# A blocked attention and two mixture layers on one core: one late exponential per half unit, the float64 conversion paused at the change of layers

## The chip, the cores and the metric

The kernel runs on 1 core of one Trainium2 chip. The metric is device microseconds from launch to end; three timed executions of the kernel before took 914.43, 926.68 and 923.3 us, median 923.3 us. A further execution was profiled.

## What is computed

Attention over blocks with 8 memory keys and a local window, then two feed-forward layers of 1536 tokens x 512. The first has four experts weighted by normalised domain probabilities and a ReLU, the second a hidden size of 2048 with a per-channel leaky slope:

```python
scores = scale * np.matmul(q_c, k_full.transpose(0, 1, 3, 2))
scores = scores - np.max(scores, axis=-1, keepdims=True)
a = np.exp(scores)
a = a / (np.sum(a, axis=-1, keepdims=True) + 1e-09)
out[:, :, c_start:c_end] = np.matmul(a, v_full)
...
h = np.maximum(x @ w1[e], 0.0)
out += p[:, e:e + 1] * (h @ w2[e])
...
h = x @ w_in
g = np.maximum(h, 0.0) + alpha * np.minimum(h, 0.0)
return (g @ w_out).astype(np.float32)
```

The weights of the second layer (`w_in`, `w_out`) arrive as float64 bit patterns and are turned into float32 on the chip.

## The kernel before

**Attention.** The work is 16 units (a batch entry and a block of 96 queries), each in two half units of 4 heads, so 32 half units, numbered 0 to 31 in the order in which they run. A half unit is a generator (`half_unit`, line 191) of four stages. Stage 1: four score products `s` on TensorE into one PSUM bank (96 queries x 4 heads x 128 keys), the next load of queries and keys, the row maximum `mx` and its scaled negative `nm` on VectorE, four exponentials `pe` on ScalarE (line 213, one for each head, reading PSUM, with `nm` as bias). Stage 2: four transposes `t` on TensorE and a copy `pt_ring` on ScalarE. Stage 3: four products `x` with the values (a column of ones gives the sums), then on VectorE `dn`, `rd` and the scaled result `xs_ring`. Stage 4: two transposes `xt` and a copy into `acc` on ScalarE; after every fourth half unit `prep_x` (line 128) makes the sums `st` and the high and low parts `xh` and `xl` of 96 columns for the products that follow. `pe`, `pt_ring` and `xs_ring` have two buffers each, used by half units in turn.

**Order.** Everything on TensorE, VectorE, ScalarE and GpSimd is kept in the order in which Python emits it (`Pinned`, line 47; line 57 is therefore the line of almost every instruction). That order comes from a planner's clock `now`, which each matmul moves on by its supposed duration. A generator that yields `LAT` is called again when `now` has passed that time; at most `LIVE` = 4 half units are open, a new one each `PACE` = 2.3. While nothing else can be run (`att_poll(force=True)`), small bf16 matmuls on a tile `warm` fill the gap (`fill`, line 92). The first 20 half units run like this; the rest are put between the matmuls of the first column tile's second product (`product`, line 448).

**Layers.** Each layer is a loop over 256 hidden channels (pair p = 0 to 15 in the first, 16 to 23 in the second) and over two column tiles of 384. `gemm1` (line 455) is seven products of six matmuls (`a`, `b`, `d`, `a`, `c`, `d`, `c`) from the sums of inputs and of weights, `gemm2` (line 542) eight outputs `y` of six, added into `acc` by VectorE (`evac`). Operands are float32 split into a high part (`xh`, `wh`, `gg`) cast by ScalarE and a low part (`xl`, `wl`, `gg`) subtracted by GpSimd, or by VectorE for p = 0 and 1 (`fast`). `prep_w` (line 298) makes the weights ahead of need; where TensorE's turn comes first, `prep_force` (line 425) emits the missing steps on the spot.

**Conversion.** `convert` (line 373) turns the second layer's weights into float32 in 32 chunks, one each 18 of the planner's clock: load into the tile tagged `fr`, five VectorE instructions on `fm` and `fw`, one on ScalarE and two on GpSimd (`fl`), a store to the DRAM tile `w2s`. `prep_w` loads the raw weights of pair p only once chunk 4(p-15) has been emitted (`conv_done`).

**Change of layers.** When `gemm2` of pair 15 has finished a column tile, `transition` (line 155) runs `prep_x` four times over it with VectorE for `st` and `xl`, while the other column tile is multiplied. The order of tiles there is written out in line 607.

Of the kernel before, what the change touches and what calls it, by code (L numbers as in the profile page):

```python
# [10 lines left out]
F32 = mybir.dt.float32  # L11
# [3 lines left out]
AF = mybir.ActivationFunctionType  # L15
ALU = mybir.AluOpType
# [4 lines left out]
BLK = 96  # L21
NCH = BLK // CH
KEYS = MEM + LEFT + BLK + RIGHT
DQ = D + NCH
NBLK = S // BLK
NU = B * NBLK
NT, DM = B * S, H * D
E, F1, F2 = 4, 1024, 2048
P = 128
# [33 lines left out]
def tile_kernel(ctx: ExitStack, tc: tile.TileContext, qk, mask, v, wa, wq, dpt, alpha, out):  # L63
    nc = tc.nc
    scale = 1.0 / float(D) ** 0.5
    pe_, dve, act, pool = (Pinned(tc, e) for e in (nc.tensor, nc.vector, nc.scalar, nc.gpsimd))

    cp = ctx.enter_context(tc.tile_pool(name="cp", bufs=1))
# [21 lines left out]
    now = [0.0]  # L90
# [34 lines left out]

    acc = xp.tile([P, KD, 2, NCOL], F32, name="acc")

    def prep_x(c0, n, fast):
        cs = slice(c0, c0 + n)
        b11, b12 = acc[:, 0:2, 0, cs], acc[:, 0:2, 1, cs]  # L130
        b21, b22 = acc[:, 2:4, 0, cs], acc[:, 2:4, 1, cs]
        st = bp.tile([P, 4, 2, n], F32, tag="st", name=f"st{c0}")
        e = dve if fast else pool
        sub = ALU.subtract
        act.copy(xh[:, 0:4, cs], acc[:, :, 0, cs])
        e.tensor_tensor(out=st[:, 0], in0=b12, in1=b11, op=sub)
        yield
        e.tensor_tensor(out=st[:, 1], in0=b22, in1=st[:, 0], op=sub)
        act.copy(xh[:, 4:6, cs], b22)
        yield  # L140
        e.tensor_tensor(out=st[:, 2], in0=b22, in1=b12, op=sub)
        pool.tensor_tensor(out=xl[:, 0:4, cs], in0=acc[:, :, 0, cs], in1=xh[:, 0:4, cs].bitcast(F32), op=sub)
        yield
        e.tensor_tensor(out=st[:, 3], in0=b21, in1=st[:, 1], op=sub)
        pool.tensor_tensor(out=xl[:, 4:6, cs], in0=b22, in1=xh[:, 4:6, cs].bitcast(F32), op=sub)
        yield
        for z in (0, 2):
            r = slice(6 + 2 * z, 10 + 2 * z)
            t_ = st[:, z:z + 2].rearrange("p a b n -> p (a b) n")
            act.copy(xh[:, r, cs], t_)  # L150
            yield
            e.tensor_tensor(out=xl[:, r, cs], in0=t_, in1=xh[:, r, cs].bitcast(F32), op=sub)
            yield
# [37 lines left out]
    def half_unit(u, half):  # L191

        hu = 2 * u + half
        tq, tv = qk_t[hu % RING], v_t[hu % RINGV // 2][:, hu % 2]
        tq = tq[:DQ]
        qv = tq[:, :QW].rearrange("p (h q) -> p h q", q=BLK)
        kv = tq[:, QW:].rearrange("p (h k) -> p h k", k=KEYS)
        vv = tv.rearrange("p (h d) -> p h d", d=D + 1)
        c, ab = divmod(u, 2)
        cols = slice(c * BLK, (c + 1) * BLK)  # L200
        hs = slice(2 * half, 2 * half + 2)
        nm = f"{u}_{half}"
        s_ps = bank(f"s{nm}").rearrange("p (h k) -> p h k", k=KEYS)
        for i in range(4):
            mm(s_ps[:BLK, i], qv[:, i], kv[:, i], n=KEYS, passes=4, start=True, stop=True)
        load_half(hu + RING)
        mx = cp.tile([P, 4], F32, tag="mx", bufs=4, name=f"mx{nm}")
        dve.tensor_reduce(out=mx[:BLK], in_=s_ps[:BLK], axis=AX.X, op=ALU.max)
        nm_ = cp.tile([P, 4], F32, tag="nm", bufs=4, name=f"nm{nm}")
        dve.tensor_scalar_mul(nm_[:BLK], mx[:BLK], -scale)  # L210
        pe = pe_t[hu % 2]
        for i in range(4):
            act.activation(
                pe[:BLK, i], s_ps[:BLK, i], AF.Exp, bias=nm_[:BLK, i:i + 1], scale=scale
            )
        yield LAT[0]
        t_ps = bank(f"t{nm}")[:, :4 * BLK].rearrange("p (h q) -> p h q", q=BLK)
        for i in range(4):
            pe_.transpose(t_ps[:, i], pe[:BLK, i], ident[:BLK, :BLK])
            now[0] += 0.085  # L220
        pt = pt_ring[:, hu % 2]
        act.copy(pt, t_ps)
        yield LAT[1]
        x_ps = bank(f"x{nm}")[:, :4 * (D + 1)].rearrange("p (h d) -> p h d", d=D + 1)
        for i in range(4):
            mm(x_ps[:BLK, i], pt[:, i], vv[:, i], n=D, passes=4, least=0.17, start=True, stop=True)
        load_v(hu + RINGV)
        dn = cp.tile([P, 4, 1], F32, tag="dn", bufs=2, name=f"dn{nm}")
        dve.tensor_scalar_add(dn[:BLK], x_ps[:BLK, :, D:D + 1], 1e-9)
        rd = cp.tile([P, 4, 1], F32, tag="rd", bufs=2, name=f"rd{nm}")  # L230
        dve.reciprocal(rd[:BLK], dn[:BLK])
        xs = xs_ring[:, hu % 2]
        dve.tensor_tensor(
            out=xs[:BLK], in0=x_ps[:BLK, :, :D], in1=rd[:BLK].to_broadcast([BLK, 4, D]),
            op=ALU.mult,
        )
        yield LAT[2]
        xt_ps = bank(f"xt{nm}")[:, :2 * BLK].rearrange("p (c q) -> p c q", q=BLK)
        xf = xs.rearrange("p h d -> p (h d)")
        for z in range(2):  # L240
            pe_.transpose(xt_ps[:, z], xf[:BLK, z * P:(z + 1) * P], ident[:BLK, :BLK])
            now[0] += 0.085
        act.copy(acc[:, hs, ab, cols], xt_ps)
        if ab == 1 and half == 1:
            for _ in prep_x(c * BLK, BLK, c < 2):
                yield 0.4

    att = {"next": 0, "start": 0.0, "done": 0, "over": set(), "live": []}

    def att_poll(force=False):  # L250

        while True:
            due = [x for x in att["live"] if x[0] <= now[0]]
            room = att["next"] < 2 * NU and len(att["live"]) < LIVE
            if due:
                x = due[0]
                try:
                    lat = next(x[1])
                    x[0] = now[0] + lat
                except StopIteration:  # L260
                    att["live"].remove(x)
                    att["over"].add(x[2])
                    while att["done"] in att["over"]:
                        att["done"] += 1
            elif room and att["start"] <= now[0]:
                g = half_unit(*divmod(att["next"], 2))
                att["start"] = now[0] + (PACE0 if force else PACE)
                att["next"] += 1
                x = [0.0, g, att["next"] - 1]
                att["live"].append(x)  # L270
                x[0] = next(g) + now[0]
            elif force:
                times = [x[0] for x in att["live"]]
                if room:
                    times.append(att["start"])
                t = min(times)
                fill(int((t - now[0]) / 0.11))
                now[0] = max(now[0], t)
                continue
            else:  # L280
                return
            if force:
                return
# [81 lines left out]
    def convert():  # L365

        for k in range(4 * NP2):
            t0 = now[0]

            def pause(t=DT_CONV):  # L370
# [254 lines left out]
    for i, (what, k) in enumerate(order):  # L625
        p, c0, n = tiles[k]
        if what == 1:
            if p == 0:
                while att["done"] < 4 * -(-(c0 + n) // BLK):
                    att_poll(force=True)  # L630
                    prep_poll()
                    if att["next"] >= 4 and not second:
                        second = True
                        load_raw(0, 1)
                        nc.sync.dma_start(nalpha, alpha)
                    if att["done"] >= 4 and not pb_t:
                        gate()
                        dve.tensor_scalar_mul(nalpha, nalpha, -1.0)
                        load_pb(0, 0, FIRST[0][1])
            if k == k0:  # L640
                stream("c", convert())
                streams["c"][0] = now[0] + 20.0
            if k + 1 < len(tiles):
                p1, d0, m = tiles[k + 1]
                if p1 < NP1 and (2 * p1 * P // F1, d0, m) not in pb_t:
                    load_pb(2 * p1 * P // F1, d0, m)
            if p >= NP1 and f"x{c0}" in streams:
                prep_force(f"x{c0}", lambda: f"x{c0}" not in streams)
            hold[0] = p == 0
            acts[k] = gemm1(p, c0, n, k % 2 if p else 0, k == final[p])  # L650
        else:
            hold[0] = False
            gemm2(p, c0, n, acts.pop(k), order[i - 1] == (1, k), k == final[p])
            if p == NP1 - 1:
                stream(f"x{c0}", transition(c0, n))
# [2 lines left out]
USE = (A11, S2, S1, A12, S3, S4, A22)  # L658
SLOTS = 10

LAT = (2.6, 1.0, 1.4)
LIVE = 4
PACE = 2.3
PACE0 = 2.3
# [80 lines left out]
```

## Time and profile before

| | |
|---|---|
| timed executions | 914.43, 926.68, 923.3 us (median 923.3) |
| profiled execution, its own time | 916.23 us |
| its span (first to last instruction) | 914.5 us |
| lies around the span | 1.7 us |
| mean granted TensorE clock | 0.972 |
| busy: PE, DVE, ACT, POOL | 870.7, 622.9, 363.0, 571.2 us |

PE is TensorE's matmuls, PEld its weight loads, DVE VectorE, ACT ScalarE, POOL GpSimd. PE is busy 95% of the span, but the share is not the same everywhere: the span falls into attention (0 to 148 us, with the first pair's products from 76.8 us on), the first layer (to 621 us), the change of layers (621 to 677 us) and the second layer. The granted clock is given as a share of 2.4 GHz, so that 0.5 is 1.2 GHz, and a mean of 0.82 over a stretch is 36% of it at the lower level.

### The profile page before, as it was taken

To read this page: it belongs to the slowest core of one execution; us is meant where nothing else is said; L and a number is where in the kernel's file an instruction comes from. 1 tells how busy PE (TensorE), PEld (TensorE's weight loads), DVE (VectorE), ACT (ScalarE), POOL (GpSimd) and SP (SyncE) were. 2 spreads that over 40 slices of the span, in tenths; PEclk is the share of its full clock that TensorE was granted. 3 is DMA by queue.
4 is the path that set the end of the run, shared out by engine and by line. 5 is a ranking of instruction groups with operands and counts; after the bars stand their busy time and mean duration, and the time that the engine had idled before them with its cause. 6 is when DMAs were issued, how large, how long until landed. Compare 5 with 4: busy or idle time off the path is not lost.

```text
span 914.5 us, 14418 instructions
## 1 busy us (share of the span) xinstructions
PE 870.7 (95%) x5211; PEld 852.5 (93%) x5211; DVE 622.9 (68%) x1232; ACT 363.0 (40%) x874; POOL 571.2 (62%) x619
## 2 busy tenths in 40 slices
PE   8888779999999999999999999998689999999998
PEld 7778668999999999999999999997579999999998
DVE  4765444676777677767766676769987767765655
ACT  4655343222323232322232232324456556454632
POOL 1134333677768776777777787767559778775521
PEclk9789888999999999999999999999889999999999
DMA  7442220022223213321232223121102221211003
GB/s 187 127 146 70 65 78 24 24 70 92 79 72 104 72 56 100 120 70 59 81 105 73 89 81 104 47 82 42 61 15 101 93 80 37 87 53 47 1 1 138
DMA packets 29353, 69.36 MB, mean 76 GB/s; under 512 B 4536, under 2 KB 12856, under 8 KB 29282
## 3 DMA queue, kind: packets, MB, share of 16 engines
q1 hardware_dynamic: 29186, 68.41, 23.2%
q8 instruction: 41, 0.67, 0.3%
q14 instruction: 30, 0.25, 0.1%
q0 software_dynamic: 96, 0.03, 0.0%
HBM read 56.87 MB, written 11.56 MB: 75 GB/s over the span
## 4 chain that ended last, share of the span: by engine, by line
PE 86%; DVE 6%; ACT 4%; issue 1%; POOL 1%; DMA 1%; SPq 0%; ACTq 0%; DVEq 0%; POOLq 0%
PE y L57 42%; PE a L57 10%; PE d L57 10%; PE c L57 10%; PE b L57 5%; PE s L57 3%; PE x L57 3%; ACT pe L57 2%; DVE st L57 2%; DVE xl L57 1%; DVE mx L57 1%; PE t L57 1%; ACT pt_ring L57 1%; DVE g L57 1%; DMA qk<-in_mask 1%
## 5 line engine op out<-in xcount | busy, mean ns | idle before, releaser
L57 PE MATMUL y<-gg,wh 128*128 128x384 f32 x1540 | 404.8, 338 | 8.2 <-POOL gg L57 3.9
L57 PEld LDWEIGHTS y<-gg,wh 128*128 128x128 f32 x1540 | 280.7, 190 | 12.2 <-POOL gg L57 6.2
L57 POOL TENSOR_TENSOR gg<-g,gg 128x384 fp32r<-128x384 f32 x192 | 198.9, 1044 | 128.9 <-ACT gg L57 105.8
L57 PE MATMUL y<-gg,wl 128*128 128x384 f32 (+1 forms) x770 | 259.9, 337 | 0.0
L57 DVE TENSOR_TENSOR acc<-y,acc 128x384 f32<-128x384 f32 x353 | 188.5, 550 | 66.8 <-PE y L57 63.6
L57 ACT CAST gg<-g 128x384 fp32r<-128x384 f32 x192 | 97.6, 511 | 168.9 <-DVE g L57 168.7
L57 PEld LDWEIGHTS y<-gg,wl 128*128 128x128 f32 x770 | 146.2, 190 | 0.0
L57 POOL TENSOR_TENSOR wl<-raw,wh 128x256 fp32r<-128x256 f32 (+1 forms) x110 | 109.2, 1003 | 50.1 <-PE b L57 43.1
L57 ACT COPY u<-a 128x384 f32<-128x384 f32 x48 | 23.0, 479 | 215.9 <-PE a L57 215.7
L57 POOL TENSOR_TENSOR wl<-s,wh 128x256 fp32r<-128x256 f32 x88 | 67.7, 777 | 5.1 <-ACT wh L57 5.0
L57 PE MATMUL c<-xh,wh 128*128 128x384 f32 x192 | 64.9, 338 | 4.3 <-DVE b L57 4.3
L57 PE MATMUL d<-xh,wh 128*128 128x384 f32 x192 | 64.8, 337 | 0.6 <-DVE t L57 0.6
L57 PE MATMUL d<-xh,wl 128*128 128x384 f32 x192 | 64.6, 336 | 0.0
L57 PE MATMUL c<-xl,wh 128*128 128x384 f32 x192 | 64.6, 336 | 0.0
L57 PE MATMUL c<-xh,wl 128*128 128x384 f32 x192 | 64.6, 336 | 0.0
L57 PE MATMUL d<-xl,wh 128*128 128x384 f32 x192 | 64.6, 336 | 0.0
L57 PE MATMUL a<-xh,wh 128*128 128x384 f32 x192 | 64.5, 336 | 0.0
L57 PE MATMUL a<-xl,wh 128*128 128x384 f32 x192 | 64.4, 335 | 0.0
L57 DVE TENSOR_TENSOR u<-b,u 128x384 f32<-128x384 f32 x48 | 26.7, 556 | 55.2 <-PE b L57 51.2
L57 PE MATMUL a<-xh,wl 128*128 128x384 f32 x192 | 64.2, 334 | 0.0
L57 POOL TENSOR_TENSOR xl<-acc,xh 128x384 fp32r<-128x384 f32 (+1 forms) x32 | 27.6, 868 | 51.5 <-ACT xh L57 51.4
L57 ACT ACTIVATE pe<-s,nm 96x128 f32<-96x128 f32 x128 | 36.1, 360 | 58.0 <-DVE nm L57 41.5
(142 smaller groups left out, 1591.2 us busy)
## 6 DMA issues: line engine op xcount, KB each, us to landing
raw<-in_wa SPq DMA_DIRECT2D x32, 512.0 KB, 3.4
fr<-in_wq SPq DMA_DIRECT2D x32, 512.0 KB, 3.4
w2s<-fl SPq DMA_DIRECT2D x32, 256.0 KB, 2.8
raw<-w2s SPq DMA_DIRECT2D x16, 512.0 KB, 3.6
qk<-in_qk SPq DMA_DIRECT2D x32, 224.0 KB, 3.4
v<-in_v SPq DMA_DIRECT2D x32, 130.0 KB, 2.1
pb<-p_dram SPq DMA_DIRECT2D x8, 384.0 KB
outT<-acc SPq DMA_DIRECT2D x15, 192.0 KB, 2.0
```

Source lines behind the costliest of these rows:

```text
L57: return self.tc.keep_in_program_order(f(*a, **kw))
```

## The change

Three things are edited. (1) In a half unit the scaled negative maximum and the four exponentials go. VectorE subtracts the maximum from all 4 x 128 scores at once, from PSUM into the `pe` buffer in SBUF; after a further yield of `LATE` = 1.5 one exponential runs in place over 96 x 512. `LAT` becomes (1.2, 1.5, 1.6). `clear` holds a half unit back until the one two before it, whose buffers it takes over, has emitted the stage that frees them. (2) `convert` begins no chunk while `change[0]` is true, from `gemm2` of tile kx-2 to `gemm2` of tile kx+1 (the change of layers). (3) In that stretch every second `prep_x` takes its `st` from the tile tagged `fr`, which the conversion otherwise uses.

```diff
-        st = bp.tile([P, 4, 2, n], F32, tag="st", name=f"st{c0}")
+        st = bp.tile([P, 4, 2, n], F32, tag="fr" if change[0] and c0 // n % 2 else "st", name=f"st{c0}")
...
-        nm_ = cp.tile([P, 4], F32, tag="nm", bufs=4, name=f"nm{nm}")
-        dve.tensor_scalar_mul(nm_[:BLK], mx[:BLK], -scale)
         pe = pe_t[hu % 2]
-        for i in range(4):
-            act.activation(
-                pe[:BLK, i], s_ps[:BLK, i], AF.Exp, bias=nm_[:BLK, i:i + 1], scale=scale
-            )
+        dve.tensor_tensor(
+            out=pe[:BLK], in0=s_ps[:BLK], in1=mx[:BLK].unsqueeze(2).to_broadcast([BLK, 4, KEYS]),
+            op=ALU.subtract,
+        )
+        yield LATE
+        act.activation(pe[:BLK], pe[:BLK], AF.Exp, scale=scale)
         yield LAT[0]
...
+    NEED = {0: 3, 2: 4, 3: 5}
+
+    def clear(hu):
+        return hu < 2 or att["stage"][hu - 2] >= NEED.get(att["stage"][hu], 0)
...
-            due = [x for x in att["live"] if x[0] <= now[0]]
-            room = att["next"] < 2 * NU and len(att["live"]) < LIVE
+            due = [x for x in att["live"] if x[0] <= now[0] and clear(x[2])]
+            room = att["next"] < 2 * NU and len(att["live"]) < LIVE and clear(att["next"])
...
         for k in range(4 * NP2):
+            yield now[0], lambda: not change[0]
...
             hold[0] = False
+            change[0] = kx - 2 <= k <= kx + 1
...
-LAT = (2.6, 1.0, 1.4)
+LAT = (1.2, 1.5, 1.6)
+LATE = 1.5
```

How the edit moves instructions is seen at three places. The first is TensorE in the second part of attention, where half units stand between the matmuls `y` of pair 0 (`s`, `t`, `x`, `xt` as above; the number behind a name counts tiles, so equal numbers are the same half unit's stage). Before:

```order
L57 MATMUL x_1_1272<-v_107,pt_ring 96x65 x4
L57 MATMUL s_1_1284<-qk_106 96x128 x4
L57 MATMUL t_0_1298<-ident,pe_110 128x96 x4
L57 MATMUL y_0_1_1_0_1270<-gg_0_0_1122,wl_0_658 128x384
L57 MATMUL xt_1_1305<-ident,xs_ring 128x96 x2
L57 MATMUL y_0_1_1_0_1270<-gg_0_0_1122,wh_0_657 128x384
L57 MATMUL y_0_0_0_0_1140<-gg_0_0_1138,wh_0_657 128x384
L57 MATMUL y_0_0_0_0_1140<-gg_0_0_1138,wl_0_658 128x384
L57 MATMUL y_0_0_0_0_1140<-gg_0_0_1138,wh_0_657 128x384
L57 MATMUL x_0_1314<-v_108,pt_ring 96x65 x4
L57 MATMUL s_0_1325<-qk_104 96x128 x4
L57 MATMUL t_1_1339<-ident,pe_111 128x96 x4
```

So `x` of one half unit was followed by the scores of the half unit two later, then by the transposes of the one between. Now:

```order
L57 MATMUL s_1_1278<-qk_105 96x128 x4
L57 MATMUL x_1_1287<-v_108,pt_ring 96x65 x4
L57 MATMUL t_0_1298<-ident,pe_110 128x96 x4
L57 MATMUL y_0_3_0_0_1149<-gg_0_0_1063,wl_0_552 128x384
L57 MATMUL y_0_3_0_0_1149<-gg_0_0_1063,wh_0_551 128x384
L57 MATMUL y_0_0_1_0_1187<-gg_0_0_1059,wh_0_551 128x384
L57 MATMUL s_0_1309<-qk_106 96x128 x4
L57 MATMUL xt_1_1318<-ident,xs_ring 128x96 x2
L57 MATMUL x_0_1325<-v_107,pt_ring 96x65 x4
L57 MATMUL t_1_1338<-ident,pe_111 128x96 x4
```

The scores of the half unit two later now stand ahead of `x`, and those of the half unit three later behind it.

The second place is ScalarE in the same stretch. Before, the exponential of the next half unit stands ahead of the copy `pt_ring` of this one:

```order
L57 ACTIVATE pe_111<-s_1_1284,nm_1_1292 96x128 x4
L57 COPY pt_ring<-t_0_1298 128x384
L57 COPY acc<-xt_1_1305 128x2x96
L57 ACTIVATE pe_110<-s_0_1325,nm_0_1333 96x128 x4
L57 COPY pt_ring<-t_1_1339 128x384
```

Now, with the exponential on `pe` in place:

```order
L57 ACTIVATE pe_111<-pe_111 96x512
L57 COPY pt_ring<-t_1_1262 128x384
L57 COPY acc<-xt_0_1268 128x2x96
L57 ACTIVATE pe_110<-pe_110 96x512
L57 COPY pt_ring<-t_0_1298 128x384
```

The copy is that of the same half unit whose exponential stands ahead of it (`pe_111` and `t_1`, `pe_110` and `t_0`).

The third place is ScalarE at the last pair's first column tile (`gemm1` of p = 23), where the conversion's later end shows. Before, all casts of that pair's weights `wh_23` stand ahead of `u`:

```order
L57 CAST wh_23_2_9488<-raw_23_9183 128x256
L57 CAST gg_22_384_9468<-g_22_384_9431 128x384
L57 CAST gg_22_384_9476<-g_22_384_9475 128x384
L57 CAST wh_23_9516<-raw_23_9246 128x512 x2
L57 COPY u_0_9566<-a_0_9558 128x384
L57 ACTIVATE g_23_0_9591<-a_0_9558 128x384
L57 ACTIVATE g_23_0_9591<-g_23_0_9591,nalpha 128x384
L57 ACTIVATE g_23_0_9610<-b_0_9568 128x384
```

Now the last three casts stand among the products' own work:

```order
L57 COPY u_0_9452<-a_0_9442 128x384
L57 CAST wh_23_5_9473<-s_9318 128x256
L57 ACTIVATE g_23_0_9481<-a_0_9442 128x384
L57 ACTIVATE g_23_0_9481<-g_23_0_9481,nalpha 128x384
L57 CAST wh_23_6_9494<-s_9318 128x256
L57 ACTIVATE g_23_0_9505<-b_0_9454 128x384
L57 ACTIVATE g_23_0_9505<-g_23_0_9505,nalpha 128x384
L57 CAST wh_23_2_9510<-raw_23_9250 128x256
```

The casts of the sixth and seventh weight sets (`wh_23_6`, `wh_23_2`) moved behind ScalarE's work on the products `a` and `b` of the same `gemm1`.

## Rows read from the trace of the kernel before

**Rows 1.** Stretches: start:end, length, busy PE, PEld, DVE, ACT, POOL, clock, DMA share, GB/s.

```profile
15.30:31.70 16.40, 13.88 (x112) 12.89 (x113) 12.41 (x36) 10.61 (x37) 1.69 (x2) 0.83 0.40 108
31.70:63.10 31.40, 27.54 (x222) 25.39 (x221) 20.75 (x62) 18.23 (x59) 7.45 (x10) 0.82 0.53 146
63.10:76.80 13.70, 10.50 (x108) 9.85 (x106) 6.65 (x20) 9.13 (x30) 5.34 (x8) 1.00 0.39 109
76.80:92.40 15.60, 13.70 (x100) 13.32 (x100) 8.42 (x21) 7.84 (x24) 7.25 (x10) 1.00 0.23 63
92.40:147.80 55.40, 44.84 (x317) 39.53 (x316) 21.69 (x64) 21.77 (x72) 15.78 (x22) 0.82 0.21 59
...
168.50:604.30 435.80, 435.80 (x2515) 435.65 (x2514) 313.78 (x589) 131.38 (x292) 321.95 (x338) 1.00 0.24 80
...
621.00:677.00 56.00, 40.89 (x182) 35.76 (x181) 52.43 (x89) 25.48 (x59) 39.61 (x40) 0.88 0.14 47
...
691.70:894.50 202.80, 202.80 (x1172) 202.80 (x1171) 134.63 (x251) 106.89 (x231) 134.79 (x145) 1.00 0.15 52
```

**Rows 2.** Waits of PE from 0 to 165 us: total, times, longest.

```profile
PE x L57 <- ACT pt_ring L57: 20.4, 17, 1.9
```

**Rows 3.** The chain that ended last, 107.7 to 112.5 us: start, us, what.

```profile
107.80 0.89 PE x L57 x8
108.70 0.92 PE s L57 x8
...
109.64 0.70 DVE mx L57
...
110.43 0.18 DVE nm L57
...
110.71 0.13 ACT pe L57
...
110.98 0.86 ACT pe L57 x3
111.84 0.37 ACT pt_ring L57
...
112.25 0.30 PE x L57
```

**Rows 4.** Groups of instructions by form: busy us, mean ns, idle before.

```profile
L57 DVE TENSOR_TENSOR acc<-y,acc 128x384 f32<-128x384 f32 x351 | 187.8, 551 | 66.4 <-PE y L57 63.3
...
L57 ACT ACTIVATE fl<-fr 128x512 f32<-128x512 uint32 x32 | 21.5, 672 | 4.4 <-POOL fl L57 4.4
```

**Rows 5.** The chain that ended last, at 146 us: twelve warm matmuls.

```profile
146.32 1.31 PE ps98.54266666666673_1721 L57 x12
```

**Rows 6.** Timeline of VectorE and of GpSimd around 625 us: start, duration.

```profile
625.02 0.55 DVE L57 TENSOR_TENSOR xl<-st,xh 128x384 fp32r<-128x384 f32 x1
...
625.96 1.17 DVE L57 TENSOR_TENSOR xl<-st,xh 128x384 fp32r<-128x384 f32 x1
...
625.23 1.48 POOL L57 TENSOR_TENSOR fl<-fl,fm 128x512 f32<-128x512 f32 x1 [1.42 <-PE a L57]
```

**Rows 7.** Stretch 621 to 677 us, tile `fm` alone: DVE busy, POOL busy, clock, DMA.

```profile
621.00:677.00 56.00, 4.37 (x7) 2.74 (x2) 0.88 0.14 47
```

**Rows 8.** The same stretch, tile `fl` alone: ACT busy, POOL busy, clock, DMA.

```profile
621.00:677.00 56.00, 0.69 (x1) 5.44 (x4) 0.88 0.14 47
```

**Rows 9.** The tile `fw` over the span: ns min/median/max, first and last start.

```profile
L57 DVE SCALAR_TENSOR_TENSOR fw<-fr,fm x32: 674/730/1349, 200.5 to 794.2; 128x512 uint32<-128x512 uint32 x32
```

**Rows 10.** ScalarE's timeline in the last pair's first tile: start, duration.

```profile
875.86 0.49 ACT L57 ACTIVATE g<-a 128x384 f32<-128x384 f32 x1 [2.64 <-PE a L57]
...
878.08 0.62 ACT L57 ACTIVATE g<-g,nalpha 128x384 f32<-128x384 f32 x1
```

**Rows 11.** TensorE's timeline there, first product with the sixth set's low part.

```profile
877.05 0.33 PE L57 MATMUL d<-xh,wl 128*128 128x384 f32 x1
```

**Rows 12.** GpSimd's low parts of weights, by form: busy us, mean ns, idle before.

```profile
L57 POOL TENSOR_TENSOR wl<-s,wh 128x256 fp32r<-128x256 f32 x88 | 67.7, 777 | 5.1 <-ACT wh L57 5.0
```

More of the change, by code (lines that the diff above doesn't have):

```diff
@@ L126, in tile_kernel @@
     acc = xp.tile([P, KD, 2, NCOL], F32, name="acc")
+    change = [False]
     def prep_x(c0, n, fast):
@@ L246, in half_unit @@
                 yield 0.4
-    att = {"next": 0, "start": 0.0, "done": 0, "over": set(), "live": []}
+    att = {"next": 0, "start": 0.0, "done": 0, "over": set(), "live": [], "stage": [0] * 2 * NU}
+    NEED = {0: 3, 2: 4, 3: 5}
+    def clear(hu):
+        return hu < 2 or att["stage"][hu - 2] >= NEED.get(att["stage"][hu], 0)
     def att_poll(force=False):
         while True:
-            due = [x for x in att["live"] if x[0] <= now[0]]
-            room = att["next"] < 2 * NU and len(att["live"]) < LIVE
+            due = [x for x in att["live"] if x[0] <= now[0] and clear(x[2])]
+            room = att["next"] < 2 * NU and len(att["live"]) < LIVE and clear(att["next"])
             if due:
@@ L257, in att_poll @@
                 try:
+                    att["stage"][x[2]] += 1
                     lat = next(x[1])
@@ L271, in att_poll @@
                 x[0] = next(g) + now[0]
+                att["stage"][x[2]] = 1
             elif force:
-                times = [x[0] for x in att["live"]]
+                times = [x[0] for x in att["live"] if clear(x[2])]
                 if room:
```

## The prediction

> **What bounds the kernel now.** I read the busy time by stretch first. In the two layers TensorE has no gap at all: 435.8 of 435.8 us and 202.8 of 202.8 us busy, at a granted clock of 1.00 [rows 1]. Nothing that the change does to other engines can make these 639 us shorter; it can only spoil them. All that is to be had lies in attention (15.3 to 147.8 us) and at the change of layers (621 to 677 us). There the clock is 0.82 to 0.88 in most stretches, and TensorE is idle besides.
>
> Next the waits. In attention TensorE waits for one thing, the copy `pt_ring` ahead of the value products: 20.4 us in 17 waits, none over 1.9 us [rows 2]. Then the chain, to see why that copy is late. From one `x` to the next, 107.80 to 112.25, is 4.45 us, and the chain goes through everything: `x` 0.89, `s` 0.92, `mx` 0.70, `nm` 0.18, the exponentials, `pt_ring` 0.37, `x` again [rows 3]. The order rows say why it is a circle: `s` of the half unit two later stands behind `x`, and its exponential stands ahead of the `pt_ring` of the half unit between. So each half unit costs one whole circle of 4.45 us, whatever TensorE could do.
>
> At the change of layers VectorE is the bound: 52.43 of 56.0 us busy, TensorE 40.89 [rows 1]. 4.37 us of VectorE and 5.44 us of GpSimd there are the conversion's [rows 7, 8].
>
> **The change, part by part.**
>
> *The subtraction.* No row shows it. `mx` reads the same 96 x 512 from PSUM in 0.70 us [rows 3]; a two-input instruction with one input in PSUM takes 0.551 us for 384 columns [rows 4]. Scaled by columns the latter gives at most 0.73 for 512. Below I bound it by 0.55, above by twice 0.70, since two-input instructions are sometimes doubled (0.55 and 1.17 us for the same `xl`) [rows 6]. It is nearest to `mx`; I take 0.69. The second `xl` began while GpSimd's `fl` of 1.48 us ran. The Trainium skill ("SBUF — State Buffer", Who interferes with whom) says that a VectorE instruction with two SBUF inputs is held by a GpSimd instruction that reads SBUF, and one with a single SBUF input is not. The rows agree for `xl`; the subtraction has one input in PSUM, so by that rule it stays near 0.69, while the doubled price would lower the gain by the 12 us worked out below.
>
> *The exponential.* Four took 1.13 us from the first's start at 110.71 (0.86 for the last three) [rows 3]. One over 512 columns lies between 0.86 and the 0.672 us of a 512-column activation [rows 4], or below that since it follows an in-place source of fewer partitions; I take 0.62, with 0.5 and 0.86 as bounds. ScalarE gets about 0.4 us free per half unit, but it is not the bound anywhere. `mx`, subtraction and exponential together (0.70 + 0.69 + 0.62) last as long as before (0.70 + 0.18 + 1.13): the change of instructions by itself gains nothing and costs VectorE 0.51 us for each half unit (0.69 for 0.18).
>
> *The order.* This is where the gain is. In the order rows of after, `x` stands ahead of the scores of the half unit three later, and each `pt_ring` behind its own exponential only. The circle becomes `x`, `s`, `mx`, subtraction, exponential, `t`, `pt_ring`, `x`: 0.89 + 0.92 + 0.70 + 0.69 + 0.62 + 0.37 [rows 3], 0.45 for four transposes (no row shows them; half of `x`'s eight matmuls) and 0.25 of gaps (what the 4.45 us leave over their parts) = 4.9 us, but now once in three half units, 1.6 us each. That is below what TensorE needs for one, so TensorE becomes the bound where VectorE isn't.
>
> *Second part of attention (76.8 to 147.8, 71.0 us).* TensorE's own work: 13.70 us at clock 1.00, and 44.84 at 0.82. A mean of 0.82 over 55.4 us is 36% at the lower level, 19.9 us, of which half (10.0) is stretch. At full clock 13.7 + 34.9 = 48.6 us. The order has 14 more warm matmuls in this part (78 for 64) at 1.31 / 12 = 0.11 us [rows 5]: 1.5 us. Floor 50 us. I take 55, since the last two or three half units have nothing beside them and still run as a chain. Gain 16 us; bounds 0 (a circle of 4.45 us stays) and 21.
>
> *First part (15.3 to 76.8, 61.5 us, half units 4 to 19).* TensorE 13.88 + 27.54 + 10.50 = 51.9 us, of it (0.34 x 16.4 + 0.36 x 31.4) / 2 = 8.4 stretch: 43.5, with 4 more warm matmuls 44. VectorE, which also prepares the first pairs' weights here: 12.41 + 20.75 + 6.65 = 39.8, plus 16 x 0.51 = 8.2: 48 us. Both floors lie close together and the order can't fill both, so I take 52. Ten more warm matmuls stand ahead of the fifth scores: 1 us. Gain 9.5 - 1 = 8.5 us; bounds 0 and 12.5. With a subtraction of 1.4 us VectorE's floor would be 59.5, and nearly all of this part's gain is gone; the second part would lose some 4 us as well: 12 us together.
>
> *Change of layers.* With the conversion paused, 4.37 us leave VectorE's chain and 5.44 us GpSimd. The second also shortens `xl` and `st`, as seen above. What is late next are ScalarE's casts `xh` and GpSimd's `xl`. The second `st` buffer gives nothing: VectorE writes `st` and reads it last, in its own order. I take 5 us; bounds 0 (another engine's chain of the same length) and 56.0 - 48.1 = 8.
>
> *Where the chunks go.* One chunk comes about every 19 us ((794.2 - 200.5) / 31) [rows 9]; nine now follow the change of layers (nine of the 32 stand behind it in the order), to about 850 us in the old time. In the second layer TensorE has no gap, with VectorE at 134.63 and GpSimd at 134.79 of 202.8 us [rows 1], so 3 more chunks of about 3.1 us of VectorE each (4.37 / 7 for one of a chunk's five instructions [rows 7]) are covered. If they were not, each would cost up to that. What isn't covered is the end: raw weights of pair 23 wait for the last chunk, and the order puts the casts of its sixth and seventh sets behind ScalarE's work on `a` and `b`. In old time `a` gets its first activation at 875.86 to 876.35 and the second (0.62, as the one at 878.08) to 876.97; then come the cast of 256 columns (at most the 0.49 of 384 columns, I take 0.4) and GpSimd's low part of 0.777: 878.15 [rows 10, 12], where TensorE wants it at 877.05 [rows 11]: 1.1 us. The seventh: ScalarE is done with `b` at 878.70, then again 0.4 + 0.78 = 879.88, wanted one set later (six matmuls of 435.8 / 2515 = 0.173 us [rows 1]), at 878.09, and the 1.1 of delay: 0.7 us more. Cost 1.8 us; bounds 0 and 5 (each of the last four sets late by cast and subtraction). Queues of DMA: the load of pair 23 stands in SP's order ahead of the last two stores, so it isn't held by them.
>
> **Sum.** -8.5 - 16 - 5 + 1.8 = -27.7 us. The profiled span was 914.5, so 886.8, and with 1.7 us around it 888.5 us against that execution's own 916.2. The median of the runs shown is 923.3, 7 us above; I add 2.5 us for such scatter: 891 us.
>
> **Rivals.** *VectorE takes over*: the subtraction costs near 1.4 us. For it: VectorE's doubled rows, and a floor of 48 us already next to TensorE's 44. Against: `acc<-y,acc`, also with one PSUM input, averages 0.551 us over 351 [rows 4], with GpSimd busy beside it. 891 + 12 = 903 us.
>
> *The circle stays*: some other pair of instructions ties each half unit to the one before in the second part, as `exp` and `pt_ring` did. For it: VectorE's and ScalarE's orders still mix half units. Against: the order rows. 891 + 16 = 907 us.
>
> *The clock goes, slower than before*: TensorE works at 1.2 GHz through attention. For it: it was at 0.82 there with TensorE busy 81 to 88% [rows 1]. Against: in the layers, without gaps, it is 1.00, and the new order has fewer gaps. Each us of full-clock work at the lower level costs 1 us more; attention has 44 + 50 = 94, and I left 4 and 5 us for all delays. It decides from 28 + 9 = 37 us of stretch, 40% of that work at the lower level (about 20% now: 18.4 of 94). At 60%, 56 - 37 = 19 us over: 935 us.
>
> *The pause does nothing*: casts and GpSimd are the chain at the change of layers. 896 us.
>
> **Chances.** Forecast with the pause's rival 0.68 (876 to 900 us: from all gains at their floors, 41.5 us less 1.8, to 9 us short of the sum). VectorE 0.13, circle 0.13, clock 0.06. The range of 876 to 911 leaves out the clock and half of the scatter. A measurement of this kernel can tell about 2%, so faster is below 904.8: the forecast and part of the VectorE case, 0.72; same 0.23; slower than 941.8: 0.05.
>
> **What would show it.** Right: `PE x <- ACT pt_ring` falls from 20.4 to under 8 us; the clock of attention is above 0.9; the last `xt` of attention at 118 to 127 us; `mx` and subtraction back to back on VectorE in 1.4 us; the change of layers some 51 us; a wait of TensorE of 1 to 2 us for `wl` or `wh` near the end. Wrong: a wait of `t` for the exponential, or of `xt` for `xs_ring`, of 1 us in each half unit; VectorE without gaps in the second part; the clock below 0.8.

## The result, and the profile after

The changed kernel took 882.35 us (median of 4 runs, 880.75 to 886.37) beside 924.99 us for the kernel before (4 runs, 914.43 to 927.32): a ratio of 0.957, 95% interval 0.949 to 0.965. Its profiled execution took 882.34 us, its span is 880.6 us, 33.9 less than before's 914.5; the sum had -27.7. A second set of 6 runs (below) gave 885.88 us and a ratio of 0.962, 0.958 to 0.966. The 924.99 us beside the first set are high for the kernel before: in the three other sets its median is 919.37, 920.9 and 920.5 us, so the gain is nearer 35 to 38 us than 43.

First the stretches after, to be read against [rows 1] (columns as there). The second part of attention now runs from 70.2 to about 121 us, and the change of layers from 594.1 to 641.6.

```profile
15.30:31.70 16.40, 13.53 (x132) 12.17 (x130) 14.63 (x46) 9.99 (x26) 1.66 (x2) 1.00 0.46 114
31.70:63.10 31.40, 28.37 (x234) 26.32 (x234) 25.07 (x61) 16.67 (x40) 8.67 (x11) 0.84 0.57 160
63.10:70.20 7.10, 6.74 (x69) 6.35 (x70) 5.02 (x12) 4.39 (x11) 3.71 (x6) 1.00 0.38 104
70.20:121.00 50.80, 49.69 (x438) 47.53 (x437) 35.41 (x87) 24.73 (x58) 23.18 (x31) 1.00 0.32 86
150.00:570.00 420.00, 420.00 (x2425) 419.85 (x2424) 303.14 (x569) 126.36 (x281) 314.05 (x329) 1.00 0.23 81
594.10:641.60 47.50, 38.75 (x187) 34.36 (x185) 44.67 (x81) 24.59 (x59) 33.72 (x36) 0.93 0.07 23
660.00:836.00 176.00, 176.00 (x1017) 176.00 (x1017) 123.94 (x239) 93.49 (x202) 129.75 (x138) 1.00 0.21 71
```

TensorE is without a gap in the layers as before. In the second part of attention it is now busy 49.69 of 50.80 us at clock 1.00. In the first part the clock is still 0.84 for 31.4 us. TensorE's waits up to 165 us, to be read against [rows 2]:

```profile
PE xt L57 <- DVE xs_ring L57: 5.7, 6, 2.0
...
PE s L57 <- ACT pt_ring L57: 0.6, 1, 0.6
```

The wait of `x` for `pt_ring` (20.4 us) is gone. What is left are 5.7 us in which TensorE waits for VectorE. The chain from 80 us on shows why: up to 88 us no step of it belongs to ScalarE or VectorE, and from `x` to `x` (80.26, 84.49, 87.18) are 3.5 us on average, with matmuls `y` of pair 0 among them, where [rows 3] had 4.45.

```profile
80.26 0.65 PE x L57 x8
80.92 0.23 PE y L57
81.15 0.88 PE s L57 x8
82.02 0.36 PE y L57 x2
82.38 0.33 PE t L57 x4
82.72 0.17 PE xt L57 x2
82.88 0.73 PE y L57 x4
83.61 0.88 PE s L57 x8
84.49 0.65 PE x L57 x8
85.14 0.34 PE t L57 x4
85.48 1.43 PE y L57 x8
86.90 0.28 PE xt L57 x2
87.18 0.65 PE x L57 x8
```

The prices, from the groups by form (busy us, mean ns, idle before):

```profile
L57 DVE TENSOR_TENSOR pe<-s,mx 96x512 f32<-96x512 f32 x32 | 22.0, 687 | 2.8 <-DVE mx L57 0.5
L57 DVE TENSOR_REDUCE mx<-s 96x4 f32<-96x512 f32 x32 | 21.9, 684 | 18.8 <-PE s L57 18.7
L57 ACT ACTIVATE pe<-pe 96x512 f32<-96x512 f32 x32 | 20.2, 630 | 14.6 <-DVE pe L57 14.6
```

Subtraction 0.687 us (0.69 was taken), exponential 0.630 (0.62).

**Where the time went.** ScalarE copies `a` into `u` once in each of the 48 `gemm1`, so its 48 starts are marks that every kernel here has. The next table gives, for each profiled execution, by how much each section between two marks is longer or shorter than in before's profile (us): from the start to the first mark (78.39 us before), to the second (151.63), the change of layers (mark 32 at 622.03 to mark 40 at 763.54), and the last pair (mark 47 at 872.74 to mark 48 at 888.34). The sections between these differ by at most 0.5 us. The median is that of the timed runs, the ratio goes against the runs of before that were timed beside it.

| kernel | first part | second part | change of layers | last pair | median, ratio (interval) |
|---|---|---|---|---|---|
| changed | -7.06 | -19.84 | -8.84 | +1.83 | 882.35, 0.957 (0.949, 0.965) |
| the same again | -3.53 | -19.82 | -7.67 | +1.83 | 885.88, 0.962 (0.958, 0.966) |
| e1_attention_only | -2.63 | -19.82 | +0.05 | 0.00 | 892.91, 0.971 (0.966, 0.976) |
| e2_pause_only | -0.78 | +8.29 | -8.85 | +1.83 | 914.20, 0.994 (0.990, 0.997) |
| e3_instr_only | -2.03 | +3.75 | +0.04 | 0.00 | 912.25, 0.994 (0.990, 0.998) |
| e4_order_only | -1.39 | -18.89 | -8.32 | +1.86 | 885.79, 0.963 (0.955, 0.970) |
| e5_sub_twice | +8.14 | -14.67 | -8.84 | +1.84 | 902.38, 0.978 (0.971, 0.985) |
| e6_one_st | -3.72 | -19.84 | -8.81 | +1.83 | 885.54, 0.961 (0.954, 0.968) |
| e7_early_chunks | -2.06 | -19.83 | -8.87 | 0.00 | 883.91, 0.959 (0.950, 0.967) |
| e8_exp_at_once | -8.98 | -19.62 | -7.66 | +1.86 | 881.36, 0.958 (0.954, 0.962) |
| e9_gate_later | -3.25 | -19.85 | -8.39 | +1.83 | 883.77, 0.960 (0.953, 0.966) |
| e10_old_order_filled | +0.11 | -2.16 | -0.95 | 0.00 | 915.46, 0.995 (0.992, 0.998) |
| e11_less_vector | -8.06 | -19.70 | -6.78 | 0.00 | 879.03, 0.956 (0.952, 0.959) |

### The profile page after: what moved, and what is told of

Read it like the earlier page. It is cut to its first block, busy times and chain, and to the rows that moved or that the text cites. A ratio compares the mean times of both kernels' runs of the same rounds, so it can differ in the third digit from the quotient of the medians.

```text
span 880.6 us, 14380 instructions
## 1 busy us (share of the span) xinstructions
PE 857.5 (97%) x5239; PEld 842.3 (96%) x5239; DVE 628.4 (71%) x1232; ACT 348.9 (40%) x778; POOL 571.8 (65%) x619
## 4 chain that ended last, share of the span: by engine, by line
PE 85%; DVE 8%; POOL 3%; issue 2%; ACT 1%; DVEq 0%; POOLq 0%; ACTq 0%
PE y L57 41%; PE d L57 11%; PE a L57 10%; PE c L57 10%; PE b L57 6%; PE s L57 2%; DVE st L57 2%; PE x L57 2%; PE t L57 1%; DVE acc L57 1%; DVE xl L57 1%; DVE pe L57 1%; POOL wl L57 1%; DVE mx L57 1%; POOL gg L57 1%
## 5 line engine op out<-in xcount | busy, mean ns | idle before, releaser
L57 DVE TENSOR_TENSOR acc<-y,acc 128x384 f32<-128x384 f32 x353 | 188.4, 551 | 65.8 <-PE y L57 63.1
L57 POOL TENSOR_TENSOR wl<-raw,wh 128x256 fp32r<-128x256 f32 (+1 forms) x110 | 110.3, 1015 | 45.6 <-PE b L57 33.1
L57 ACT CAST wh<-raw 128x256 fp32r<-128x256 f32 (+1 forms) x120 | 55.7, 487 | 0.6 <-PE a L57 0.6
```

What stands on the lines that cost most here:

```text
L57: return self.tc.keep_in_program_order(f(*a, **kw))
```

## The experiments

### The two edits apart (e1, e2)

The diff of e1 against the changed kernel; e2 is the kernel before with just these lines (and the line that sets `change[0]`).

```diff
-        st = bp.tile([P, 4, 2, n], F32, tag="fr" if change[0] and c0 // n % 2 else "st", name=f"st{c0}")
+        st = bp.tile([P, 4, 2, n], F32, tag="st", name=f"st{c0}")
...
-            yield now[0], lambda: not change[0]
```

> The changed kernel with the conversion not paused and one buffer of sums, so edit 1 alone. If the two parts add up as the shifts between the traces do (attention -26.9 us, change of layers -8.8, end +1.8), attention's 26.9 us stay and the other 7.0 go: about 889 us, span 887.6, with no stall of TensorE before the last pair. Rival, the gain at the change of layers came with attention or by chance of the clock: 880 to 884 us.

> The kernel before with edits 2 and 3 alone. Adding up: a span of 914.5 - 8.8 + 1.8 = 907.5 us, some 7 us less than before in the same rounds, the change of layers 8.8 us shorter and 1.8 us of stall at the last pair. The prediction's own term was 5 for the first of these, which would leave -3 us. Rival, the pause does nothing there: +2 us.

e1 keeps the second part's gain whole and has neither the change of layers' nor the end's shift; e2 has these two alone, each within 0.01 us of what the changed kernel shows. So the parts add up by place. In the medians e1 is 26.5 us below before, e2 5.2, together 31.6; the second set of the changed kernel is 34.6 below the runs of before beside it. e1's 892.91 is 4 above what was expected; its first part has 4.4 us less of a gain than the changed kernel's first profile, with the same order (clock 0.67 for 0.84 in 31.7 to 63.1 us). The profiled execution of e2 has a second part 8.3 us longer than before's profile with the same order of attention: its clock from 76.8 to 150 us was 0.65, where before's was 0.86, and TensorE was busy 51.72 of the 55.40 us from 92.4 to 147.8 at 0.56. So the time of the old order depends on how low the clock falls there.

### Instructions or order (e3, e4, e8)

e3 puts the new instructions into the old order, e4 the old instructions into the new one, e8 takes the exponential's late place away:

```diff
# e3, against before
-        nm_ = cp.tile([P, 4], F32, tag="nm", bufs=4, name=f"nm{nm}")
-        dve.tensor_scalar_mul(nm_[:BLK], mx[:BLK], -scale)
...
-        for i in range(4):
-            act.activation(
-                pe[:BLK, i], s_ps[:BLK, i], AF.Exp, bias=nm_[:BLK, i:i + 1], scale=scale
-            )
+        dve.tensor_tensor(
+            out=pe[:BLK], in0=s_ps[:BLK], in1=mx[:BLK].unsqueeze(2).to_broadcast([BLK, 4, KEYS]),
+            op=ALU.subtract,
+        )
+        act.activation(pe[:BLK], pe[:BLK], AF.Exp, scale=scale)
# e4, against the changed kernel: the same the other way round, with yield LATE ahead of the four
# e8, against the changed kernel
-LAT = (1.2, 1.5, 1.6)
-LATE = 1.5
+LAT = (2.7, 1.5, 1.6)
+LATE = 0.0
```

> The kernel before with the subtraction and one exponential in the place of the scaled negative and four, in the old order with the old delays (no late yield, no holding back). The prediction's claim: 2.01 us for 2.01 us, so the circle stays at some 4.4 us for a half unit, TensorE still waits about 20 us for pt_ring, and the time is that of before within 4 us. Rival, the instructions bring half of attention's gain: 13 us less.

> The changed kernel with the scaled negative and the four exponentials put back, in the new places (the negative behind the maximum, the exponentials behind the late yield). If the order brings the gain, the time is that of the changed kernel within 5 us (877 to 887): VectorE has 0.51 us less for each half unit, ScalarE about 0.5 more. Rival, one exponential is needed, since ScalarE or the longer hold on the scores' bank takes over: 895 us or more.

> The changed kernel with the exponential emitted straight behind the subtraction (LATE 0, LAT (2.7, 1.5, 1.6), the same sum of delays), so that on ScalarE it stands ahead of copies of older half units, as pt_ring or acc, and holds them until the subtraction is done. If the late place is part of what breaks the circle, the time is 5 us or more above the changed kernel, and TensorE waits for pt_ring or acc again (over 5 us together). Rival, the order on TensorE is enough: within 4 us.

e3's chain still goes once around for each half unit: from `x` at 109.94 to `x` at 114.33 are 4.39 us, where [rows 3] had 4.45 (both at the upper level of the clock).

```profile
109.94 0.89 PE x L57 x8
110.83 0.92 PE s L57 x8
...
111.77 0.70 DVE mx L57
...
112.56 0.70 DVE pe L57
...
113.29 0.63 ACT pe L57
113.92 0.37 ACT pt_ring L57
...
114.33 0.89 PE x L57 x8
```

From 118.7 us on the clock is 0.50 and `x` follows `x` after 5.9 us: `x` and `s` now take 1.54 and 1.77 us of the circle, and TensorE's own work is nearly as long as the circle, so that the chain goes through TensorE alone up to 130.5 us and around the circle from there on.

```profile
118.70:147.00 28.30, 27.56 (x137) 24.12 (x138) 10.28 (x25) 7.20 (x19) 5.72 (x8) 0.50 0.12 37
```

The median of e3 is 7 us below before (interval 2 to 9), a little more than the 4 that were allowed. TensorE's waits for `pt_ring` are 13.1 instead of 20.4 us in its profile, but the clock of 76.8 to 150 us was 0.72 there, so the profile doesn't say what these 7 us are. e4 shows the other half: with the four old exponentials the new order has nearly all of the gain (885.79 us, ratio 0.963). So it is the order that pays, and the subtraction isn't needed for it. e8 fell out against my first theory: with the exponential at once the waits for `pt_ring` come back as 2.7 us in 5 waits, `xs_ring`'s fall to 4.2, and the time is that of the changed kernel.

```profile
PE xt L57 <- DVE xs_ring L57: 4.2, 4, 1.4
PE x L57 <- ACT pt_ring L57: 2.7, 5, 0.7
```

What carries the gain is therefore where the stages stand on TensorE (the delays of `LAT` and the holding back by `clear`); which of these two was not tried, since `clear` also keeps a buffer from being overwritten before it is read.

### Gaps and the clock (e10, e9)

```diff
# e10, against before
+        x_b = bank(f"x{nm}")
+        x_ps = x_b[:, :4 * (D + 1)].rearrange("p (h d) -> p h d", d=D + 1)
+        if hu >= 16:
+            for _ in range(8):
+                pe_.matmul(x_b[:, 264:], warm[:, :P], warm[:, :248], start=True, stop=True)
# e9, against the changed kernel
-                    if att["done"] >= 4 and not pb_t:
+                    if att["done"] >= 14 and not pb_t:
```

> The kernel before with eight warm matmuls of 248 columns put ahead of the value products of half units 16 to 31, in the unused columns of their own bank, so that the wait for pt_ring (1.2 us on average, 1.9 at most) is filled and the circle of 4.45 us stays. If TensorE's gaps draw its clock down, the clock of 76.8 to 147 us rises from 0.82 (0.65 in the kernel with the pause alone) to over 0.95 and that part takes 60 to 67 us instead of 71, the matmuls' own cost included where no wait covers them. Rival, the clock falls for another reason: it stays under 0.85 and the part takes 71 us or more.

> The changed kernel with the normalising of the domain probabilities (eight small VectorE instructions, 1.3 us in one block at 30 us) emitted after the 14th finished half unit instead of the 4th. The block stands on the chain, ahead of 2 us of idle TensorE, behind which its clock falls to 0.5 for some 10 us. If the idle time draws the fall, the clock of 15 to 70 us is over 0.95 and the first product starts 4 to 6 us earlier. If the fall comes anyway, only the 1.3 us are won, or nothing.

The stretch 92.4 to 147.8 us of e10, to be read against the row of that stretch in [rows 1]:

```profile
92.40:147.80 55.40, 48.38 (x430) 42.92 (x431) 21.69 (x64) 24.12 (x79) 18.78 (x27) 1.00 0.21 60
```

The clock goes from 0.82 to 1.00, so the gaps did draw it down (over the whole span, the ten runs of e10 have a mean clock of 0.973 to 0.989, the 17 of before beside them 0.953 to 0.973). But the part from mark 1 to mark 2 gets shorter by 2.16 us only, not by 4 to 11, because the circle stays, as e10's chain shows (`x16` are the eight warm matmuls and the eight of `x`):

```profile
107.80 1.82 PE x L57 x16
109.62 0.92 PE s L57 x8
...
113.19 0.89 PE x L57 x8
```

`x` itself starts some 0.9 us into the first piece, at 108.7, and 4.5 us later again. So a part of 73 us whose TensorE works at full clock throughout is still 71 us long, and the 10 us of "stretch" in the account of the old order were not 10 us to be had from the clock alone. The 2.2 us are net: where no wait covers them, the warm matmuls cost up to 0.9 us per half unit, and this was not separated. They are also measured against one profile of before. The same order took 81.53 us there in e2's profile, at clock 0.65, so the clock costs 2 us in one execution and 10 in another; in the medians e10 is 5 us below before. At an equal clock of 1.00 the old order takes 71.07 us (e10) and the new one 53.40: these 17.7 us are the order's, apart from what the warm matmuls cost.

e9 moves eight small VectorE instructions away that stood on the chain at 30 us. Four-us stretches of the changed kernel, then of e9:

```profile
28.00:32.00 4.00, 2.29 (x24) 1.97 (x21) 3.72 (x15) 0.95 (x2) 0.00 (x0) 1.00 0.49 132
32.00:36.00 4.00, 3.75 (x23) 3.58 (x24) 2.18 (x5) 1.32 (x3) 0.00 (x0) 0.62 0.53 134
36.00:40.00 4.00, 4.00 (x25) 4.00 (x24) 2.07 (x6) 1.00 (x2) 0.00 (x0) 0.50 0.77 212
```

```profile
28.00:32.00 4.00, 3.20 (x31) 2.69 (x30) 3.90 (x11) 1.54 (x5) 0.00 (x0) 1.00 0.40 101
32.00:36.00 4.00, 3.94 (x41) 3.62 (x38) 3.21 (x7) 2.32 (x5) 0.00 (x0) 1.00 0.74 231
36.00:40.00 4.00, 3.64 (x38) 3.27 (x37) 3.75 (x8) 2.98 (x8) 2.00 (x2) 1.00 0.53 132
40.00:44.00 4.00, 2.76 (x31) 2.60 (x28) 3.83 (x11) 2.08 (x5) 0.00 (x0) 1.00 0.49 143
44.00:48.00 4.00, 3.34 (x17) 3.04 (x18) 3.86 (x12) 1.10 (x3) 0.00 (x0) 0.57 0.73 181
```

TensorE's gap at 28 us (2.29 of 4 us busy) is smaller (3.20), and the fall of the clock behind it is gone; but it comes behind the next gap (2.76 at 40 us), and the time is the same. Removing one of several gaps moved the fall and won nothing that can be measured.

### VectorE as the bound (e5, e11)

```diff
# e5, against the changed kernel: the subtraction once more behind itself
+        dve.tensor_tensor(
+            out=pe[:BLK], in0=s_ps[:BLK], in1=mx[:BLK].unsqueeze(2).to_broadcast([BLK, 4, KEYS]),
+            op=ALU.subtract,
+        )
# e11, against the changed kernel
-            for _ in prep_x(c * BLK, BLK, c < 2):
+            for _ in prep_x(c * BLK, BLK, c < 1):
-        fast = p <= 1
+        fast = p <= 0
-T_CONV = 18.0
+T_CONV = 17.0
```

> The changed kernel with the subtraction issued twice (the same instruction, the same tile), so VectorE pays 1.38 us for each half unit, as in the rival VectorE takes over. The rival's price was 12 us: the first pair's products start about 8 us later and the last xt 4 more. If TensorE has slack cover instead (the start of the first product is bound by the clock and by TensorE's own work), under 4 us.

> The changed kernel with less for VectorE in the first part of attention (sums of the second column group and weights of pair 1 on GpSimd, which is busy 10 of the 47 us before 63), and a chunk each 17 of the planner's clock. If VectorE bounds the first part, its idle time of TensorE (5.7 us of waits for xs_ring) and the fall of the clock behind it lessen: the first product starts 2 to 6 us earlier, and 1.8 us of stall at the end go: 874 to 880 us. Rival, GpSimd's slower instructions come too late or double VectorE's: no gain or a loss.

> The changed kernel once more, beside the others of this call: 882 us within 3; the first product's start between 71 and 77 us by the clock of the first part, the rest of the shifts as in its first profile (19.8, 8.8 and -1.8 us, each within 0.5).

e5 is 15 to 20 us slower than the changed kernel (its ratio 0.978 against 0.962 and 0.957, of 921 us), more than the rival's 12. The first mark is 10 to 15 us later than in the changed kernel's executions with the same order, the second part 5.2 longer. TensorE's waits for `xs_ring` double (12.1 us for 5.7). From 15.3 us to the first mark VectorE is busy 57.5 us, where the five profiles with the changed kernel's order have 45.6 to 46.7, and the clock is 0.76, where they have 0.81 to 0.91. How the delay is shared between VectorE's time and the clock is not separated. From 31.7 to 63.1 us VectorE is busy 27.20 of 31.40 us, at a clock of 0.69:

```profile
31.70:63.10 31.40, 24.98 (x172) 22.95 (x171) 27.20 (x68) 11.88 (x29) 2.59 (x3) 0.69 0.48 135
```

e11, which bundles three edits, goes the other way. It took 879.03 us (6 runs, 878.07 to 881.31) where the changed kernel beside it took 885.88 (6 runs, 880.87 to 887.0). In its profile the first mark is 4.5 us earlier than in the second profile of the changed kernel, and the stall at the end is gone. GpSimd's load in 31.7 to 63.1 us doubles to 17.87 us, and TensorE waits for `xs_ring` 2.8 us:

```profile
31.70:63.10 31.40, 30.77 (x246) 28.59 (x246) 21.34 (x48) 17.14 (x41) 17.87 (x24) 0.78 0.60 160
```

That VectorE bounds the first part is also what the changed kernel's chain says: from 39.7 to 51.4 us it holds no step of another engine. Whether the busy time counts or the length of each half unit's way through VectorE was not separated; e5 lengthens both.

e11 is the best version measured here. The two intervals to before just overlap (0.952 to 0.959, 0.958 to 0.966), and the first runs of the changed kernel (882.35) lie between, so a gain of 3 to 7 us is likely and its size not settled.

The second set of runs of the changed kernel missed two of its expectations: 885.88 us is 3.9 above 882, and its change of layers is 7.67 us shorter, not 8.8; the clock in 598 to 646 us was 0.86, where the first execution had 0.93 in 594.1 to 641.6. Over all kernels with the pause this section gained 6.8 to 8.9 us.

### The change of layers and the end (e6, e7)

e6 takes the second `st` buffer back, e7 is `T_CONV` 17 alone (both lines stand in diffs above).

> The changed kernel with one buffer of sums at the change of layers; the conversion still paused. The prediction held that the second buffer gives nothing, since VectorE writes and reads st in its own order: the change of layers is then 8.8 us shorter than before, as with it, within 0.5. Rival, ScalarE's casts of st hold the next st back: 2 to 5 us of the 8.8 are lost.

> The changed kernel with a chunk of the conversion each 17 instead of 18 of the planner's clock, so that pair 23's casts stand ahead of its products again. If the stall at the last pair is the late weights', its 1.8 us go (shift from pair 22 to pair 23 zero), all else is unchanged: 880.5 us. Rival, denser chunks cost as much at another place: 882 or more.

e6: -8.81 us without the buffer, -8.84 with it. The buffer gives nothing, and the pause alone (e2) gives -8.85. The conversion's own VectorE instructions were 4.37 us [rows 7]. Besides them the 16 `xl` on VectorE became shorter (columns: stretch, length, busy, clock, DMA, GB/s). Before, in the changed kernel, and in its second profile:

```profile
621.00:678.00 57.00, 14.55 (x16) 0.88 0.13 46
```

```profile
594.10:643.00 48.90, 10.59 (x16) 0.93 0.06 22
```

```profile
597.60:647.20 49.60, 12.34 (x16) 0.86 0.06 22
```

That is 4.0 us less in the first profile and 2.2 in the second. Little of it is the conversion's `fl` holding up an `xl`. An `xl` with no GpSimd instruction beside it takes 0.54 to 0.55 us. Before, nine of the 16 took 0.90 to 1.41, but only two of these nine stand beside `fl` (one is in [rows 6]), together 1.4 us above 0.54 each. The others stand beside GpSimd's `gg`, `wl` and `xl`, which the layers themselves need. They can still do it with the conversion paused, as in the second profile (start, duration):

```profile
608.30 1.42 DVE L57 TENSOR_TENSOR xl<-st,xh 128x384 fp32r<-128x384 f32 x1
608.30 2.27 POOL L57 TENSOR_TENSOR gg<-g,gg 128x384 fp32r<-128x384 f32 x2
```

So 4.4 us are shown as the conversion's own and up to 1.4 as its neighbours'. The rest came as, with other times, fewer `xl` met GpSimd's other work: what they take beside it above 0.54 us each is 4.5 us before, 1.9 in the first profile and 3.6 in the second. VectorE's busy time up to the end of the sixteenth `xl` falls by 7.4 us (53.43 in 621 to 678 before, 46.07 in 594.1 to 643 after). But section and `xl` do not go together us for us: e8 has only 9.85 us of `xl` and gains 7.65.

e7: the end's 1.83 us vanish with the weights ready a little earlier. In the changed kernel TensorE's waits from 836 to 850 us are:

```profile
PE d L57 <- ACT wh L57: 0.5, 1, 0.5
PE c L57 <- POOL wl L57: 0.2, 1, 0.2
PE d L57 <- POOL wl L57: 0.2, 1, 0.2
```

ScalarE there, ahead of the sixth set's products (start, duration):

```profile
840.12 0.49 ACT L57 ACTIVATE g<-a 128x384 f32<-128x384 f32 x1 [2.33 <-PE a L57]
840.65 0.62 ACT L57 ACTIVATE g<-g,nalpha 128x384 f32<-128x384 f32 x1
841.17 0.39 ACT L57 CAST wh<-s 128x256 fp32r<-128x256 f32 x1
```

The cast of the sixth set stands behind both activations of `a`, as read from the order. The matmuls' own waits are 0.9 of the 1.83 us; the weight loads, which also wait for the late set, no longer hide behind the products before them. The expected 880.5 us didn't come: e7's median of 883.91 lies between the changed kernel's two (882.35 and 885.88). Its profiled first part is 5.0 us longer than in the changed kernel's first profile, so 1.8 us are less than that part scatters, and the place alone shows them.

## Why the prediction was right, step by step

**The time.** 891 was forecast, 882.35 came; 876 to 911 holds it, and faster by more than 2% is what was held likeliest. The sum was -27.7 us against the profiled execution, -33.9 is measured, and -29.2 in the changed kernel's second profile. That the sum came so close has luck in it: in these two profiles the first part gave 1.4 and 5.0 us less than forecast, the second part 3.8 more in both, the change of layers 3.8 and 2.7 more. The rest of the distance is the 2.5 us that were added for scatter, with the wrong sign: they were taken over from the kernel before, whose second part scatters with its clock (73.2 us from mark 1 to mark 2 in its profile, 81.5 in e2's with the same order), while the new order takes 53.4 there in each of six profiles. Of the signs that were named, the wait for `pt_ring` (none left), the last `xt` (120.7 us), `mx` and subtraction (1.37 us) and the stall at the end came as forecast; the clock of attention is above 0.9 in all but the stretch from 31.7 to 63.1 us. The change of layers, named at some 51 us, took 47 to 49.

**The prices** were right to 0.01 us. All 32 subtractions take 0.686 to 0.689 us, GpSimd busy beside them or not. The exponential's 0.62 was partly luck: it lies below both rows named for it, for a reason (in place, fewer partitions) that no row or run shows.

**The order.** Right, and shown: new instructions in the old order keep a circle of 4.39 us (e3), old instructions in the new order have the gain (e4), and at equal clock the new order is 17.7 us shorter in the second part (e10). That each half unit costs one whole circle of 4.45 us, "whatever TensorE could do", holds only while the clock is up: at 0.50 the circle takes 5.9 us, since `x` and `s` are part of it (e3). The prediction said that the instructions gain nothing; measured they have 7 us of 919 with an interval of 2 to 9, so this was not quite right, and what the 7 us are stays open. The late place of the exponential, which the order rows seemed to make important, is not needed (e8).

**Second part**, -16 forecast, -19.8 measured. The floor of 50 us was right (49.69 us busy). The allowance of 5 us above it was too much, 3.4 are used (53.4).

**First part**, -8.5 forecast, -2.1 to -7.1 measured in five executions with this order (e1, e6, e7 and the two of the changed kernel). The step that was mis-sized is "of it 8.4 stretch: 43.5", which took the whole of the lower clock as gone. It is not gone: the clock from 31.7 to 63.1 us is 0.84 in the first profile and 0.67 in the second, which by the prediction's own reckoning is 5.0 and 10.4 us of stretch. VectorE bounds here, as the prediction's two floors close together allowed, and its chain leaves TensorE gaps. How much falls behind them differs between executions of the same program, and that goes with most of what scatters now.

**VectorE takes over** was a rival with the right mechanism and too low a price (12; 15 to 20 in e5). Its first part took VectorE's floor as the time, with nothing for delays or for a lower clock: 8 us, where e5 shows 10 to 15. It did not happen because the subtraction is not doubled.

**The circle stays** and **the clock goes** fell: 3.5 us from `x` to `x`, and a clock of 1.00 through the second part. In the first part the clock did go in some executions (0.67 for 31.4 us in the second profile).

**Change of layers**, -5 forecast, -8.8 measured (-6.8 to -8.9 over the executions). Mis-sized: the prediction named the shorter `xl` and gave it no price beyond 0.6 us; it measured 4.0 and 2.2 us in two profiles. The reason named, GpSimd's `fl`, accounts for 1.4 us of that at most; the other slow `xl` stood beside GpSimd's own work for the layers, and why fewer met it with the pause is not settled beyond the shift in time. `st`, named with `xl`, did not get shorter. The Trainium skill ("SBUF — State Buffer", Who interferes with whom) says that a VectorE instruction with two SBUF inputs contends with a GpSimd instruction that reads SBUF; the trace agrees in that `xl`, with two inputs in SBUF, takes 0.54 us undisturbed and up to 1.42 beside GpSimd's `gg`, while the subtraction, with one of its inputs in PSUM, never leaves 0.69. The second `st` buffer was rightly costed at nothing (e6).

**The end**, +1.8 forecast, +1.83 measured, in each execution that has the pause and chunks each 18, and zero where chunks come each 17 (e7). That it agrees so closely has luck in it: the forecast had 1.1 and 0.7 for two sets, the trace shows waits of the matmuls of 0.67 and 0.2 and the remainder in weight loads.

## What to carry to other kernels

Where the chain of waits goes through every engine once per item, look in the order for the pair of instructions that ties one item to the one before, and cost the new order by how many items share one circle; cheaper instructions inside the circle brought little here (7 us of 919). TensorE's lower clock comes with its gaps, and where a latency sets the pace, the clock given back only shortens TensorE's share of it: the old order's second part took 81.5, 73.2 and 71.1 us at clocks of 0.65, 0.86 and 1.00, the new order 53.4. A background stream that shares VectorE's chain costs its own instructions (4.4 us here) and the neighbours that it holds up itself (1.4 us). Look at each slow neighbour for the instruction beside it before the rest is put down to the stream: here most of it was GpSimd's other work.

## What the runs showed that was not expected

- The same order of attention has a first part that differs by 5 us from one execution to the next (mark 1 at 71.33 to 76.33 us in five profiles, 71.33 and 74.86 in the changed kernel's two), and the clock goes with it: 0.84 to 0.67 in 31.7 to 63.1 us. From 48 to 52 us TensorE is busy 2.17 of 4 us in the first profile, and no fall follows; in the second it is busy 2.62 us there, and the clock falls to 0.50 behind it. What decides is not settled here.
- Filling the gaps of the old order brought the clock from 0.82 to 1.00 and the time down by half a per cent only (0.995, 0.992 to 0.998), while in e2's profile, at 0.56, the same order kept TensorE busy 51.72 of the same 55.40 us and took longer.
